# Bits of the first layer's weights in the weight pools' own tiles, values in 128-row tiles, and an order planned with transfers in a row

## The chip, the cores and the metric

The kernel runs on one core of one Trainium2 chip. The metric is the device time of one execution in microseconds, so less is better. Before the change three runs took 1063.34 to 1065.43 us, with a median of 1064.94.

The core has five engines with an instruction stream each: PE (matmuls, with weight loads shown apart as PEld), DVE and ACT (elementwise), POOL, and SP, which in this kernel only issues transfers. Instructions of one engine run in the order in which they were written; engines wait for each other through semaphores.

## What is computed

Linear attention of 4 batches with 8 heads, 576 tokens and 64 columns, and behind it two multilayer perceptrons (MLPs) on its 2304 tokens.

```python
def phi(x):
    proj = np.einsum('bhsd,df->bhsf', x, w_phi)
    proj = proj - np.max(np.abs(proj), axis=-1, keepdims=True)
    return np.concatenate([np.exp(proj), np.exp(-proj)], axis=-1)
q_p, k_p = (phi(q), phi(k))
kv = np.einsum('bhsf,bhsd->bhfd', k_p, v)
z = np.sum(k_p, axis=2)
num = np.einsum('bhsf,bhfd->bhsd', q_p, kv)
den = np.einsum('bhsf,bhf->bhs', q_p, z)[..., None] + 1e-06
x = num / den                               # [2304, 512] after the heads are joined
...
h = x @ w_in                                # first MLP, 512 -> 2048 -> 512
x = (h * (1.0 / (1.0 + np.exp(-h)))) @ w_out
h = np.maximum(x @ w_in, 0.0)               # second MLP, weights of its own
return h * h @ w_out
```

The MLPs' weights come as 64-bit floats.

## The kernel before

**Work.** Heads are taken in pairs, so a batch j has four pairs p. The tokens of a batch are two blocks of 288, eight blocks in all. Each MLP is cut into 16 chunks of 128 hidden columns: for a block i and a chunk c, 12 matmuls make `h` (L887), ACT and DVE turn it into a high and a low half (`gh`, `gl`), and 12 matmuls add to the four accumulators `o` (L932). Layer 0 runs blocks 0 to 7 and layer 1 follows with blocks 0 to 7; names end in layer, block and chunk, so h0_7_0 is layer 0, block 7, chunk 0. In the text "chunk 0" and "chunk 15" without a block are those of layer 0, block 0. Most matmuls use numbers split into a high half, rounded to the format of the faster matmul, and a low half, the remainder (`hi_act` on ACT, L326, and `lo_on`, L330).

**Keys and values** (`keys_of`). The keys `kr` of a pair are projected (`pk`, L560) in five token tiles of KT = 116 rows (the last of 112), grouped as two, two and one. DVE takes the largest magnitude of each row (L565). In batch 0 DVE then subtracts it (`kd`, L571) and ACT takes both exponentials of a whole group (`kp`, L648). In batch 1 ACT negates the maximum (L582) and takes the exponentials straight from the projection, 128 columns at a time with the maximum as bias (L634), and DVE subtracts nothing. Batches 2 and 3 work with split numbers (L593, L621). The values `v` are loaded into columns of a tile in which POOL has first set a column of ones behind each group of 64 (L507, L510): 116 rows of ten pieces of 64 numbers. `pkv` (L664 for batches 0 and 1) is the product with the exponentials, and `kv` its copy.

**Queries** (`queries_of`), for a block and a pair: load `qr` (L730), project (`pq`, L749 to L752), copy to `qp` (L755), reduce over partitions on POOL (L762), subtract (L768), two exponentials `qe` (L780), the product `pn` with kv (L814), copy `qn` (L817), the denominators through three small transfers (`rr` L829, `rd` L836, `qb` L839), and the quotient `x` (L852) with its two halves, the input of the block's chunks.

**Weights** (`w_conv`, `w_split`). Half a chunk of weights, 128 x 1024 words, is loaded into a raw buffer `wr` (L404). ACT takes the magnitude of the upper words (L407), DVE makes the 32-bit number in four steps (L413, L415, L419, L423), and `w_split` writes its halves into the chunk's tile `w`. There are three raw buffers (`NRAW`), shared with the values of batches 2 and 3, and eight tiles `w` in the pool `wp` for chunks 0 to 7; chunks 8 to 15 have the pool `wq`, which opens when the buffers of the first attention close. The second layer's weights are made during blocks 3 to 7 of the first, go out to `w2d` and come back as `w2f`.

**Order.** `Plan` is a list scheduler which runs before the program is written. Each operation has a key (its due time in chunks), a planned duration, and buffers to take and give back; at each moment an engine gets the ready operation with the smallest key that `safe` allows. What comes out is the order in which instructions are written. Keys come from a table (`P`) and from the calls of `want` at the end: `k0s`, `q0s`, `q0`, `w0`, `ws` for the start, `k1`, `k`, `qo`, `qe` for later batches, `W2A`, `W2B` for the second layer's weights. Attention on PE is put ahead of the MLP by 132.7 chunks, and the MLP's work on ACT and DVE ahead of the attention's by 106.06. A transfer is planned as SP's time `max(600, kb * 1024 / 330)` and a latency of 2000 ns. On the chip SP issues all transfers from one queue.

## Time and profile before

| | |
|---|---|
| median of three runs | 1064.94 us |
| the profiled execution | 1062.18 us |
| its span, first to last instruction | 1060.4 us |
| mean granted TensorE clock | 0.977 |
| moved by transfers | 88.39 MB, mean 83 GB/s |
| shortest packets | 30816 of 67387 under 512 bytes |

Views used below: the page's shares and slices; a table of stretches (busy time of each engine between two moments, then the granted clock, the busy share of the 16 DMA engines and GB/s); the timeline (start, duration, engine, line, operation, output and inputs, how many; in brackets the idle time ahead of it and what ended it); groups of instructions by line and shape (count, busy us, mean ns, idle us before them); and waits (who waited for whom: us in all, times, longest). "SPq" is SP's queue of transfers.

### The profile page before, as it was taken

To read this page: it belongs to the slowest core of one execution; us is meant where nothing else is said; L and a number is where in the kernel's file an instruction comes from. 1 tells how busy PE (TensorE), PEld (TensorE's weight loads), DVE (VectorE), ACT (ScalarE), POOL (GpSimd) and SP (SyncE) were. 2 spreads that over 40 slices of the span, in tenths; PEclk is the share of its full clock that TensorE was granted. 3 is DMA by queue.
4 is the path that set the end of the run, shared out by engine and by line. 5 is a ranking of instruction groups with operands and counts; after the bars stand their busy time and mean duration, and the time that the engine had idled before them with its cause. 6 is when DMAs were issued, how large, how long until landed. Compare 5 with 4: busy or idle time off the path is not lost.

```text
span 1060.4 us, 19152 instructions
## 1 busy us (share of the span) xinstructions
PE 1019.5 (96%) x7424; PEld 992.0 (94%) x7424; DVE 629.7 (59%) x1278; ACT 550.0 (52%) x1369; POOL 75.6 (7%) x56
## 2 busy tenths in 40 slices
PE   7879798998999999999999999999999999999998
PEld 5649687998999999999999999999999999999998
DVE  3889879776657756898977688232323233333232
ACT  4755776776867767876644465232323232332222
POOL 2130002120002300031100000000000000000000
PEclk8989988999999999999999999999999999999999
DMA  6455462213201122237355694010101010100000
GB/s 171 109 141 152 134 171 78 74 41 76 61 23 51 54 56 80 74 113 218 112 177 175 215 318 156 1 45 2 45 1 45 2 46 1 46 1 24 1 24 23
DMA packets 67387, 88.39 MB, mean 83 GB/s; under 512 B 30816, under 2 KB 43232, under 8 KB 67296
## 3 DMA queue, kind: packets, MB, share of 16 engines
q1 hardware_dynamic: 67296, 87.17, 27.9%
q8 instruction: 58, 0.95, 0.4%
q14 instruction: 33, 0.27, 0.1%
HBM read 69.17 MB, written 17.90 MB: 82 GB/s over the span
## 4 chain that ended last, share of the span: by engine, by line
PE 74%; DMA 10%; DVE 10%; ACT 3%; issue 2%; SPq 1%; POOL 0%; ACTq 0%; DVEq 0%
PE h L887 32%; PE o L932 32%; DMA wr<-w 3%; PE pn L814 3%; PE pkv L621 2%; DMA qb<-rd 2%; PE pkv L664 1%; DVE wc L419 1%; DVE wc L423 1%; DMA rd<-rr 1%; PE pk L560 1%; ACT kp L634 1%; DMA rr<-qn 1%; DVE x L852 1%; SPq L502 1%
## 5 line engine op out<-in xcount | busy, mean ns | idle before, releaser
L887 PE MATMUL h<-x,w 128*128 128x288 f32 x3072 | 455.1, 297 | 6.7 <-DVE w L330 2.0
L932 PE MATMUL o<-gh,w 128*128 128x288 f32 x2048 | 456.7, 297 | 4.2 <-ACT gh L326 3.4
L887 PEld LDWEIGHTS h<-x,w 128*128 128x128 f32 x3072 | 425.5, 190 | 9.4 <-issue 2.7
L932 PEld LDWEIGHTS o<-gh,w 128*128 128x128 f32 x2048 | 345.6, 189 | 5.7 <-ACT gh L326 4.9
L932 PE MATMUL o<-gl,w 128*128 128x288 f32 x1024 | 303.2, 296 | 1.9 <-DVE gl L330 1.8
L330 DVE TENSOR_TENSOR gl<-a,gh 128x288 fp32r<-128x288 f32 x256 | 122.3, 478 | 167.6 <-ACT gh L326 167.0
L326 ACT CAST gh<-a 128x288 fp32r<-128x288 f32 x256 | 111.7, 437 | 199.0 <-PE o L932 148.7
L932 PEld LDWEIGHTS o<-gl,w 128*128 128x128 f32 x1024 | 193.4, 189 | 2.9 <-DVE gl L330 2.6
L904 DVE TENSOR_TENSOR a<-h,a 128x288 f32<-128x288 f32 x128 | 58.4, 456 | 108.6 <-ACT a L895 108.6
L895 ACT ACTIVATE a<-h 128x288 f32<-128x288 f32 x128 | 52.5, 410 | 117.4 <-PE h L887 117.0
L762 POOL PARTITION_ALL_REDUCE qm<-qp x32 | 73.1, 2303 | 319.2 <-ACT qp L755 178.7
L900 DVE SCALAR_TENSOR_TENSOR a<-a,h 128x288 f32<-128x288 f32 x128 | 57.6, 450 | 29.9 <-ACT a L893 29.2
L407 ACT ACTIVATE wc<-wr 128x512 f32<-128x512 f32 x64 | 43.2, 678 | 46.6 <-DMA wr<-w 46.2
L893 ACT ACTIVATE a<-h 128x288 f32<-128x288 f32 x128 | 53.3, 416 | 12.9 <-PE h L887 12.7
L423 DVE SCALAR_TENSOR_TENSOR wc<-wr,wc 128x512 int32<-128x512 int32 x64 | 46.1, 720 | 0.5
L419 DVE SCALAR_TENSOR_TENSOR wc<-wr,wc 128x512 int32<-128x512 int32 x64 | 45.8, 715 | 0.5
L593 ACT ACTIVATE ke<-pk,mx 116x128 f32<-116x128 f32 (+1 forms) x160 | 46.0, 402 | 0.0
L780 ACT ACTIVATE qe<-qp 128x576 f32<-128x576 f32 x64 | 41.6, 681 | 6.5 <-DVE qp L768 5.3
L664 PEld LDWEIGHTS pkv<-v,kp 116*128 116x128 f32 (+1 forms) x320 | 41.1, 210 | 1.4 <-issue 0.6
L814 PE MATMUL pn<-qh,kv 128*65 128x288 f32 x192 | 41.8, 294 | 0.0
L664 PE MATMUL pkv<-v,kp 116*128 116x128 f32 (+1 forms) x320 | 41.4, 293 | 0.0
L413 DVE TENSOR_SCALAR wc<-wc 128x512 f32<-128x512 f32 x64 | 28.9, 454 | 19.3 <-ACT wc L407 18.9
(83 smaller groups left out, 958.7 us busy)
## 6 DMA issues: line engine op xcount, KB each, us to landing
wr<-w SPq DMA_DIRECT2D x64, 512.0 KB, 5.1
w2d<-wc SPq DMA_DIRECT2D x32, 256.0 KB, 2.9
w2f<-w2d SPq DMA_DIRECT2D x32, 256.0 KB, 4.9
qr<-qT SPq DMA_DIRECT2D x56, 144.0 KB, 3.1
v<-v SPq DMA_DIRECT2D x16, 290.0 KB
kr<-kT SPq DMA_DIRECT2D x16, 288.0 KB, 3.8
qb<-rd SPq DMA_DIRECT2D x32, 144.0 KB, 3.2
x2d<-y SPq DMA_DIRECT2D x32, 144.0 KB, 2.0
```

The lines of the kernel that those rows point to most:

```text
L326: nc.scalar.copy(out=dst, in_=src)
L330: e.tensor_tensor(out=dst, in0=src, in1=hi.bitcast(F32), op=ALU.subtract)
L419: nc.vector.scalar_tensor_tensor(out=b, in0=lo, scalar=29, in1=b, op0=ALU.logical_shift_right, op1=ALU.bitwise_or)
L423: nc.vector.scalar_tensor_tensor(out=b, in0=hi, scalar=-(1 << 30), in1=b, op0=ALU.bitwise_and, op1=ALU.bitwise_or)
L664: nc.tensor.matmul(get(ps)[:, o:o + 128], get(kps[2 * g + s])[:nt, 2 * i + a], get(vt)[:nt, c:c + 128], start=t == 0 and a == 0 and s == 0 ...
L762: nc.gpsimd.partition_all_reduce(get(mx), get(pr).rearrange("p a t -> p (a t)"), 128, bass.bass_isa.ReduceOp.absmax)
L814: nc.tensor.matmul(get(ps)[:D1, :HB], w, get(e)[:, t], start=x == 0, stop=x == len(ops) - 1)
L887: nc.tensor.matmul(get(ps)[:, :HB], a, x[:, cc], start=k == 0, stop=k == 3 * ND - 1)
L893: nc.scalar.activation(out=a, in_=get(ps)[:, :HB], func=AF.Tanh, scale=0.5)
L900: nc.vector.scalar_tensor_tensor(out=a, in0=a, scalar=1.0, in1=get(ps)[:, :HB], op0=ALU.add, op1=ALU.mult)
L904: nc.vector.tensor_tensor(out=a, in0=get(ps)[:, :HB], in1=a, op=ALU.mult)
L932: nc.tensor.matmul(get(acc)[:, :HB], a, g, start=c == 0 and x == 0, stop=c == NC - 1 and x == 2)
```

## The change

*Bits in the weight pools.* For chunks 0 to 4 and 8 to 12 of layer 0 both halves of the raw words land in a tile of the pool that later holds the chunk's `w` (`w_tile("bits", c)`, 128 x 2 x 1024 words, shown as `wbits`). Other halves use raw buffers as before.

*Values.* KT is 128 (the last tile has 64 rows). The host lays v out with room for the ones, one row of 650 numbers for each of 128 partitions; the load is contiguous, and POOL sets the ones behind it.

*Batch 0 without a subtraction.* `bx` = 0 gives batch 0 the path of batch 1 (`direct`).

*Order.* The planner issues a transfer in 640 ns, lets all transfers pass one after the other at 240 bytes per ns, and adds 1500 ns. Loads of keys, and queries behind the keys of their pair, keep their order (`behind`). The keys sit in one table, `KEYS`, with new numbers. Line numbers from 23 on rise by up to 23 (L330 is L337 there, L510 is L531, L560 is L582, L634 is L656).

```diff
 ND = DM // 128
-KT = 116
+KT = 128
 NKT = 5
...
         self.allocs, self.frees, self.state = [], [], 0
+        self.behind = None
...
     LAT = {"PE": 450, "SP": 150}
-    DMA_LAT = 2000
+    DMA_ISSUE, DMA_LAT, DMA_RATE = 640, 1500, 240.0
...
         if unit and engine == "PE":
-            key -= 132.7
+            key -= KEYS["pe"]
         if not unit and engine in ("ACT", "DVE"):
-            key -= 106.06
+            key -= KEYS["el"]
         o = Op(len(self.ops), key, engine, cost, emit, unit)
...
         busy = dict.fromkeys(engines, 0.0)
-        events, now, left = [], 0.0, len(self.ops)
+        events, now, left, dma_free = [], 0.0, len(self.ops), 0.0
         self.active = []
...
                     if e == "SP":
-                        busy[e] = now + o.cost
-                        end = now + o.cost + self.DMA_LAT
+                        busy[e] = now + self.DMA_ISSUE
+                        dma_free = max(dma_free, busy[e]) + o.cost * 1024 / self.DMA_RATE
+                        end = dma_free + self.DMA_LAT
                     else:
...
     def allowed(self, o):
-        return not o.allocs or self.safe(o)
+        return not (o.behind and not o.behind.state) and (not o.allocs or self.safe(o))
...
 def dma(kb):
-    return max(600, kb * 1024 / 330.0)
+    return kb
...
 MM, MM256 = 132, 117
+
+
+KEYS = {
+    "k0s": 6.03, "q0s": 11.22, "q0": 7.53, "w0": 41.79, "ws": 3.48, "we": -10.51, "q1": 19.08, "qo": 5.92,
+    "qs": 0.92, "k1": 29.08, "k": 15.38, "ks": 0.85, "qe": -5.28, "w2a": 51.96, "w2b": 2.48, "bx": 0,
+    "pe": 114.63, "el": 100.63, "wl": 3.76, "kl": 3.74, "vl": -5.21, "ql": 3.88, "g2": 2.17,
+}
...
     nc = tc.nc
-    P = {
-        "k0s": 8.2, "q0s": 5.98, "q0": 7.67, "w0": 36.83, "ws": 3.47, "we": 1.51, "q1": 13.83, "qo": 4.11, "qs": 0.47, "k1": 27.16, "k": 15.28,
-        "ks": 1.3, "qe": 8.44,
-    }
+    P = KEYS
     NT, NRAW, NATT, NG, NU = 14, 3, 2, 3, 4
     NW, NE, NEU = 8, 28, 11
-    W2A, W2B = 51.14, 3.33
+    W2A, W2B = P["w2a"], P["w2b"]
     WARM = 4
-    JF, BX = 2, 1
+    JF, BX = 2, P["bx"]
     EW = 14
+    NWR = 5
     NX, NXK = 1, 2
...
     op(T0 - 99, "DVE", 200, blank, w=["blank"])
-    op(T0 - 99, "SP", dma(128), phi_load, r=["blank"], w=["wraw"])
+    op(T0 - 99, "SP", dma(64), phi_load, r=["blank"], w=["wraw"])
     op(T0 - 99, "POOL", 1500, phi_zero, w=["wbl0", "ident"])
...
         u.early = layer == 0 and 2 * c + part < EW
-        raw = Buf("raw", lambda: rp.tile([128, 512, 2], I32, tag="raw", name="wr" + n), None)
+
+        if layer == 0 and c % (NC - NW) < NWR:
+            raw = w_tile("bits", c)
+            words = lambda: get(raw)[:, part]
+        else:
+            raw = Buf("raw", lambda: rp.tile([128, 2 * 512], I32, tag="raw", name="wr" + n), None)
+            words = lambda: get(raw)
         f = slot("wc" + n, u, (128, 512))
...
         def load():
-            src = (w1, w2)[layer][c, :, part * 512:(part + 1) * 512].bitcast(I32)
-            nc.sync.dma_start(out=get(raw).rearrange("p n two -> p (n two)"), in_=src)
+            nc.sync.dma_start(out=words(), in_=(w1, w2)[layer][c, :, part * 512:(part + 1) * 512].bitcast(I32))
+
+        def halves():
+            return words().rearrange("p (n two) -> p n two", two=2)
         def mag():
-            nc.scalar.activation(out=get(f), in_=get(raw)[:, :, 1].bitcast(F32), func=AF.Abs)
+            nc.scalar.activation(out=get(f), in_=halves()[:, :, 1].bitcast(F32), func=AF.Abs)
...
             t, b = get(f), get(f).bitcast(I32)
-            lo, hi = get(raw)[:, :, 0], get(raw)[:, :, 1]
+            lo, hi = halves()[:, :, 0], halves()[:, :, 1]
             if i == 0:
...
         r = [(("c", 0, hold // NC, hold % NC), "h")] if layer else []
-        op(key - 4, "SP", dma(512), load, r=r, w=[(k, 0)], bufs=[raw])
+        op(key - P["wl"], "SP", dma(512), load, r=r, w=[(k, 0)], bufs=[raw])
         op(key, "ACT", act(512), mag, r=[(k, 0)], w=[(k, 1)], bufs=[raw, f], unit=u)
...
-    def w_split(layer, c, part, f, u, key, engine):
-        k = ("wf", layer, c, part)
-        if part == 0:
+    def w_tile(layer, c):
+        if (layer, c) not in wch:
             first = c < NC - NW
...
                 "w" if first else "wq",
-                lambda: (wp if first else late_pool()).tile([128, 4, 512], F32R, tag="w", name=f"w{layer}_{c}"), None
+                lambda: (wp if first else late_pool()).tile(
+                    [128, 4, 512] if layer in (0, 1) else [128, 2, 1024], F32R if layer in (0, 1) else I32, tag="w",
+                    name=f"w{layer}_{c}"
+                ), None
             )
-        w = wch[layer, c]
+        return wch[layer, c]
+
+    def w_split(layer, c, part, f, u, key, engine):
+        k = ("wf", layer, c, part)
+        w = w_tile(layer, c)
...
-    kvs = {}
+    kvs, loads = {}, {}
...
         def v_load():
-            nc.sync.dma_start(out=values()[:, :, :D], in_=v[j * NP + p].rearrange("k t a d -> k (t a) d"))
+            nc.sync.dma_start(out=get(vt), in_=v[j * NP + p])
...
-        op(key - 4, "SP", dma(288), load, w=[(K, "raw")], bufs=[raw], unit=u)
+        loads[K] = op(key - P["kl"], "SP", dma(288), load, w=[(K, "raw")], bufs=[raw], unit=u)
+        loads[K].behind = loads.get(("k", (j * NP + p - 1) // NP, (p - 1) % NP))
         parts = [raw]
...
                bufs=[raw, hi, lo], unit=u)
-        op(key - 3, "POOL", 200, ones, r=[(K, "raw" if whole else "lo")] if split else [], w=[(K, "one")], bufs=[vt])
-        op(key - 3, "SP", dma(290), v_load, r=[(K, "one")], w=[(K, "v")], bufs=[vt])
+        op(key - P["vl"], "SP", dma(325), v_load, r=[(K, "raw" if whole else "lo")], w=[(K, "v0")], bufs=[vt])
+        op(key - P["vl"], "POOL", 200, ones, r=[(K, "v0")], w=[(K, "v")], bufs=[vt])
...
                 if g == 0:
-                    op(key, "ACT", act(NKT * 2 * D1), v_hi, r=[(K, "v"), "kvs"], w=[(K, "vh")], bufs=[vt] + vs)
+                    op(key, "ACT", act(NKT * 2 * D1), v_hi, r=[(K, "v"), "kvs"] + [("kt", x) for x in range(JF * NP)], w=[(K, "vh")], bufs=[vt] + vs)
                     op(key, "DVE", dve(NKT * 2 * D1), v_lo, r=[(K, "v"), (K, "vh")], w=[(K, "vl")], bufs=[vt] + vs)
...
         else:
-            op(key, "PE", 4 * NKT * 2 * MM256, kv_mm, r=[(K, "v")] + [((K, g), "e", s) for g in range(3) for s in range(2)],
-               w=[(K, "t")], bufs=[ps, kv, vt] + kps, unit=u)
+            op(key, "PE", 4 * NKT * 2 * 113, kv_mm, r=[(K, "v")] + [((K, g), "e", s) for g in range(3) for s in range(2)],
+               w=[(K, "t"), ("kt", j * NP + p)], bufs=[ps, kv, vt] + kps, unit=u)
         if kv_one:
...
-        op(key - 4, "SP", dma(288), load, w=[(Q, "raw")], bufs=[raw], unit=u)
+        op(key - P["ql"], "SP", dma(144 if whole else 288), load, w=[(Q, "raw")], bufs=[raw], unit=u).behind = loads[K]
+        loads[Q] = plan.ops[-1]
         if not whole:
...
-            op(key + 3.18, "PE", 3 * MM, gemm2, r=W + [(C, "gh"), (C, "gl")], w=[("acc", L, i, d)],
+            op(key + P["g2"], "PE", 3 * MM, gemm2, r=W + [(C, "gh"), (C, "gl")], w=[("acc", L, i, d)],
                bufs=[acc, gb, w])
...
     qT = np.asarray(inputs["q"]).reshape(B, NP, 2, 2, HB, D).transpose(0, 3, 1, 5, 2, 4).reshape(B * 2 * NP, D, 2 * HB)
-    vv = np.zeros((B * NP, NKT * KT, 2, D), v.dtype)
-    vv[:, :S] = v.transpose(0, 2, 1, 3)
-    vv = vv.reshape(B * NP, NKT, KT, 2, D).transpose(0, 2, 1, 3, 4)
+    vv = np.zeros((B * NP, NKT * KT, 2, D1), v.dtype)
+    vv[:, :S, :, :D] = v.transpose(0, 2, 1, 3)
+    vv = vv.reshape(B * NP, NKT, KT, 2 * D1).transpose(0, 2, 1, 3).reshape(B * NP, KT, NKT * 2 * D1)
```

The start of SP's queue, before the change (`kr`, `qr`, `v` with batch or block and pair; `wr` with layer, chunk and half):

```order
L502 DMA kr0_0_109<-kT 128x576
L346 DMA wbl_93<-w_phi 64x128 x2
L730 DMA qr0_0_119<-qT 64x576
L510 DMA v0_0_121<-v 116x10x64
L502 DMA kr0_1_126<-kT 128x576
L510 DMA v0_1_123<-v 116x10x64
L730 DMA qr0_1_140<-qT 64x576
L502 DMA kr0_2_147<-kT 128x576
L730 DMA qr0_2_157<-qT 64x576
L502 DMA kr0_3_172<-kT 128x576
L730 DMA qr0_3_182<-qT 64x576
L404 DMA wr0_0_0_196<-w1 128x1024
```

and with it:

```order
L523 DMA kr0_0_109<-kT 128x576
L523 DMA kr0_1_112<-kT 128x576
L353 DMA wbl_93<-w_phi 64x128 x2
L752 DMA qr0_0_121<-qT 64x576
L523 DMA kr0_2_123<-kT 128x576
L523 DMA kr0_3_125<-kT 128x576
L531 DMA v0_0_127<-v 128x650
L752 DMA qr0_1_129<-qT 64x576
L531 DMA v0_1_135<-v 128x650
L752 DMA qr0_2_140<-qT 64x576
L752 DMA qr0_3_149<-qT 64x576
L416 DMA wbits_0_153<-w1 128x1024
```

The keys of all four pairs now stand ahead of the values, and the first bits, five halves in a row, come at the same place in the queue.

ACT's first rows behind the preparation of the projection, before the change (`kp` with batch, pair, group and sign):

```order
L648 ACTIVATE kp0_0_0_0_159<-kd0_0_0_149 116x512
L648 ACTIVATE kp0_0_0_1_165<-kd0_0_0_149 116x512
L755 COPY qp0_0_174<-pq0_0_0_153 128x288
L755 COPY qp0_0_174<-pq0_0_1_161 128x288
L648 ACTIVATE kp0_0_1_0_184<-kd0_0_1_170 116x512
L648 ACTIVATE kp0_0_1_1_190<-kd0_0_1_170 116x512
L648 ACTIVATE kp0_0_2_0_200<-kd0_0_2_177 112x256
L648 ACTIVATE kp0_0_2_1_204<-kd0_0_2_177 112x256
```

and with it:

```order
L604 ACTIVATE mx0_0_0_151<-mx0_0_0_151 128x4
L656 ACTIVATE kp0_0_0_0_160<-pk0_0_0_137,mx0_0_0_151 128x128 x4
L656 ACTIVATE kp0_0_0_1_172<-pk0_0_0_137,mx0_0_0_151 128x128 x4
L604 ACTIVATE mx0_0_1_158<-mx0_0_1_158 128x4
L604 ACTIVATE mx0_0_2_170<-mx0_0_2_170 64x2
L656 ACTIVATE kp0_0_1_0_190<-pk0_0_1_146,mx0_0_1_158 128x128 x4
L656 ACTIVATE kp0_0_1_1_198<-pk0_0_1_146,mx0_0_1_158 128x128 x4
L656 ACTIVATE kp0_0_2_0_211<-pk0_0_2_155,mx0_0_2_170 64x128 x2
L656 ACTIVATE kp0_0_2_1_216<-pk0_0_2_155,mx0_0_2_170 64x128 x2
```

Each exponential of a group became four, or two, with a negation ahead, and the copies of the first query moved behind the exponentials of pair 1.

DVE's rows around the end of block 6 of layer 0, from the last low half of block 7's x on; before the change, where the row of its chunk 0 stands 76 rows further on:

```order
L330 TENSOR_TENSOR x1_7_6945<-x7_3_7005,x0_7_6944 128x288
L423 SCALAR_TENSOR_TENSOR wc1_7_0_6958<-wr1_7_0_6908,wc1_7_0_6958 128x512
L330 TENSOR_TENSOR gl0_6_0_7023<-a0_6_0_7021,gh0_6_0_7022 128x288
L413 TENSOR_SCALAR wc1_7_1_6996<-wc1_7_1_6996 128x512
L415 TENSOR_SCALAR wc1_7_1_6996<-wc1_7_1_6996 128x512
L900 SCALAR_TENSOR_TENSOR a0_6_1_7060<-a0_6_1_7060,h0_6_1_7008 128x288
L419 SCALAR_TENSOR_TENSOR wc1_7_1_6996<-wr1_7_1_6947,wc1_7_1_6996 128x512
```

and with it, where that row is among these:

```order
L337 TENSOR_TENSOR x1_7_7001<-x7_3_7662,x0_7_7000 128x288
L337 TENSOR_TENSOR gl0_6_14_7657<-a0_6_14_7655,gh0_6_14_7656 128x288
L438 SCALAR_TENSOR_TENSOR wc1_15_1_7646<-wr1_15_1_7575,wc1_15_1_7646 128x512
L923 SCALAR_TENSOR_TENSOR a0_6_15_7696<-a0_6_15_7696,h0_6_15_7673 128x288
L337 TENSOR_TENSOR gl0_6_15_7698<-a0_6_15_7696,gh0_6_15_7697 128x288
L923 SCALAR_TENSOR_TENSOR a0_7_0_7731<-a0_7_0_7731,h0_7_0_7712 128x288
L337 TENSOR_TENSOR x1_8_7739<-x2r0_0_7693,x0_8_7738 128x576
L337 TENSOR_TENSOR gl0_7_0_7733<-a0_7_0_7731,gh0_7_0_7732 128x288
```

The conversions of the second layer (`wc1`, `w1`) that stood between the two rows have moved ahead of the first.

## The prediction

> **What bounds the kernel now.** I read the page first: the shares of the engines, then the slices.
>
> ```profile
> PE 1019.5 (96%) x7424; PEld 992.0 (94%) x7424; DVE 629.7 (59%) x1278; ACT 550.0 (52%) x1369; POOL 75.6 (7%) x56
> ...
> PE   7879798998999999999999999999999999999998
> ...
> DVE  3889879776657756898977688232323233333232
> ```
>
> PE is busy for 96% of the span, but the slices show two stages: up to the seventh or eighth slice of 26.5 us PE has holes while DVE is at 7 to 9 tenths, and after that PE has none. The table by stretches says how much is to be had in each.
>
> ```profile
> 0.00:82.00 82.00, 65.52 (x309) 48.09 (x310) 56.26 (x113) 46.15 (x100) 19.63 (x22) 0.85 0.53 139
> 82.00:186.00 104.00, 91.06 (x588) 84.19 (x587) 89.83 (x179) 71.35 (x195) 7.45 (x5) 0.91 0.45 134
> 186.00:300.00 114.00, 110.78 (x841) 110.24 (x840) 78.83 (x159) 82.86 (x224) 11.56 (x9) 0.99 0.24 59
> 300.00:600.00 300.00, 296.63 (x2258) 294.18 (x2256) 226.32 (x452) 195.72 (x494) 37.00 (x20) 1.00 0.38 113
> 600.00:1060.00 460.00, 455.53 (x3438) 455.30 (x3437) 178.47 (x379) 153.94 (x357) 0.00 (x0) 1.00 0.15 49
> ```
>
> Columns are the length, then busy PE, PEld, DVE, ACT, POOL, the granted clock, DMA share and GB/s. PE is idle for 16.5 us before 82, 12.9 us up to 186, and after that for 3.2, 3.4 and 4.5 us, the last at the very end of the program. So the span is the time of chunk 15 of the first block, the point where this front ends, plus a row of matmuls that hardly waits. What sets that point is read from the instructions around it.
>
> ```profile
> 82.14 0.44 DVE L900 SCALAR_TENSOR_TENSOR a<-a,h 128x288 f32<-128x288 f32 x1
> ...
> 182.34 0.68 DVE L330 TENSOR_TENSOR w<-wc,w 128x512 fp32r<-128x512 f32 x1
> ...
> 186.15 0.44 DVE L900 SCALAR_TENSOR_TENSOR a<-a,h 128x288 f32<-128x288 f32 x1
> ```
> ```profile
> 183.62 4.94 PE L887 MATMUL h<-x,w 128*128 128x288 f32 x36
> ```
>
> The weight half that chunk 15 needs ends on DVE at 183.02, and 0.6 us later its matmuls start and run on without a gap. 82.14 and 186.15 are DVE's first instruction on chunk 0 and on chunk 15. **DVE is the bound of the front**: it must convert all sixteen chunks of w1 beside the attention, and it is idle for 25.7 us before 82 and 14.2 us after. Everything below is counted at these two instructions.
>
> **The change, part by part.** *No subtraction in batch 0.* It takes twelve DVE instructions away and gives ACT exponentials of 128 columns for those of 512 and 256.
>
> ```profile
> L571 DVE TENSOR_TENSOR kd<-pk,mx 116x512 f32<-116x512 f32 x8 | 5.5, 685 | 0.1
> L571 DVE TENSOR_TENSOR kd<-pk,mx 112x256 f32<-112x256 f32 x4 | 1.6, 406 | 0.0
> ```
> ```profile
> 22.81 1.15 ACT L648 ACTIVATE kp<-kd 116x512 f32<-116x512 f32 x2 [0.91 <-DVE kd L571]
> ...
> 109.17 0.19 ACT L582 ACTIVATE mx<-mx 116x4 f32<-116x4 f32 x1
> 109.39 2.17 ACT L634 ACTIVATE kp<-pk,mx 116x128 f32<-116x128 f32 x8
> ```
>
> DVE loses 5.5 + 1.6 = 7.1 us. On ACT eight short exponentials take 2.17 us where two long ones took 1.15, and a negation of 0.2 us comes before them: +1.2 us for a group of two tiles, and about half of it for the last tile, so +3.1 us for a pair and +12.4 us for four, all of it before chunk 0.
>
> *Loads.* The loads of v occupy the transfers far longer than their size.
>
> ```profile
> 57.25 0.70 SPq L510 DMA_DIRECT2D v<-v  x1
> 58.34 4.59 SPq L829 DMA_DIRECT2D rr<-qn  x1
> ```
> ```profile
> 243.00:247.00 4.00, 4.00 (x34) 4.00 (x32) 1.38 (x2) 0.70 (x2) 0.00 (x0) 1.00 0.28 48
> ```
> ```profile
> kr<-kT SPq DMA_DIRECT2D x16, 288.0 KB, 3.8
> ```
>
> Behind a v the next issue stands for 4.59 us where it takes 0.5 otherwise, and while v alone is on the way (243 to 247) only 0.28 of the DMA engines are busy, at 48 GB/s. In 128 rows of 2600 bytes v has the form of the keys, 288 KB in 3.8 us, so I take the stalls as gone. What they cost the bound is bounded by who waits:
>
> ```profile
> ACT wc L407 <- DMA wr<-w: 25.8, 15, 4.1
> ```
> ```profile
> SPq L404 <- DVE wc L423: 59.5, 18, 6.5
> ```
> ```profile
> DVE wc L413 <- ACT wc L407: 6.6, 5, 4.6
> ```
> ```profile
> 11.03 3.48 PE L560 MATMUL pk<-wbl,kr 128*116 128x256 f32 x10 [2.47 <-DMA kr<-kT]
> ```
>
> In the first 200 us ACT waits 25.8 us for weight bits (15 times, 4.1 at most), and SP 59.5 us for DVE to give a raw buffer back. With five more tiles in each pool the first loads are queued without such a wait, so a load no longer stands behind the conversion that frees its buffer. The 25.8 us are ACT's, though, and DVE, which is the bound, waited for those ACT instructions for 6.6 us; PE waited 2.47 us for the second keys, which were queued behind the first v. Their worth lies between nothing and DVE's whole idle time in the front, 40 us; I take it in the two stretches below, nearer to nothing. The memset of the ones now stands behind v's landing on POOL, which costs POOL's next reduction up to one landing, 3.8 us, and nothing where POOL is idle (19.6 of 82 us busy). The tiles of 128 keys are five as before, with as many matmuls; time goes with columns in these rows (685 ns for 512, 406 for 256), so that edit costs nothing, and the planner's new rules add no instruction, only order.
>
> *Up to chunk 0.* The new order puts more in front of it: on DVE 16 conversion steps, 3 low halves of w, 2 subtractions of a query and 4 small ones more, and 12 kd fewer.
>
> ```profile
> L413 DVE TENSOR_SCALAR wc<-wc 128x512 f32<-128x512 f32 x64 | 28.9, 454 | 19.3 <-ACT wc L407 18.9
> ...
> L423 DVE SCALAR_TENSOR_TENSOR wc<-wr,wc 128x512 int32<-128x512 int32 x64 | 46.1, 720 | 0.5
> ...
> L768 DVE TENSOR_TENSOR qp<-qp,qm 128x576 f32<-128x576 f32 x32 | 26.7, 840 | 5.7 <-POOL qm L762 5.6
> ...
> L330 DVE TENSOR_TENSOR w<-wc,w 128x512 fp32r<-128x512 f32 x32 | 22.7, 709 | 2.5 <-ACT w L326 2.4
> ```
>
> Half the steps cost 454 and half 720 ns: 9.4 us; with 2.1 for w (709 each), 1.7 for the subtractions, 1.3 for the small ones and 7.1 off, DVE has 7.4 us more, 63.7 us. Its idle time I work out by place. Until its first reduction, at 10.07, nothing changes (about 9 us idle):
>
> ```profile
> 10.07 0.69 DVE L565 TENSOR_REDUCE mx<-pk 116x4 f32<-116x512 f32 x1
> ```
>
> Then it has seven reductions (0.69 us each, the two of half the width 0.4: 4.3) and waits for ACT, whose row now begins with both first pairs: 40 exponentials by 0.27 us, 6 negations, 2 copies of a query and the first magnitude from 11 us on, so to about 24.6: 10 us idle.
>
> ```profile
> L407 ACT ACTIVATE wc<-wr 128x512 f32<-128x512 f32 x64 | 43.2, 678 | 46.6 <-DMA wr<-w 46.2
> L780 ACT ACTIVATE qe<-qp 128x576 f32<-128x576 f32 x64 | 41.6, 681 | 6.5 <-DVE qp L768 5.3
> ...
> L755 ACT COPY qp<-pq 128x288 f32<-128x288 f32 x64 | 24.1, 403 | 8.1 <-PE pq L752 4.6 <-PE pq L749 3.0
> ```
>
> The magnitude is 0.68 and a copy 0.4 us in these rows. The 32 exponentials of pairs 2 and 3 (8.7 us) stand ahead of the next magnitudes in the same way; I allow 4 us. 63.7 + 23 = **87 us**, 5 later than 82.
>
> *Chunk 0 to chunk 15.* By the orders DVE has 273 instead of 289 instructions before chunk 15: the 12 kd, one low half of a query, two subtractions of a query and one low half of w fewer, 10.2 us. As 7.4 us more stand before chunk 0, 17.6 us fewer stand between. Neighbours overlap a little, so 16 us of busy time: 89.8 - 16 = 74, and with 13 us idle, about as before, 87. PE allows no less than 85: its 91.1 us lose 8 matmuls of pn (4.2 us) to the time before chunk 0 and 11 others (1.5 us) to the time after. Chunk 15 comes at 87 + 87 = 174 instead of 186: **-12**. The 1.5 us are paid later.
>
> *Behind it.* The stalls after v go here too; the holes around them are within the 3.2 us of PE, of which I take 1. Against it stands the order of blocks 5 and 6. From the first chunk of block 5 to that of block 7 DVE has 231 instructions instead of 188, and the last low half of block 7's x stands five rows before DVE's first instruction on that block's chunk 0, where it stood 76 rows before it.
>
> ```profile
> 440.00:490.00 50.00, 49.88 (x380) 49.45 (x380) 42.83 (x83) 36.38 (x89) 11.45 (x5) 1.00 0.43 125
> 490.00:540.00 50.00, 48.60 (x359) 47.35 (x359) 43.28 (x91) 29.79 (x69) 7.29 (x3) 1.00 0.54 161
> ```
> ```profile
> 524.41 0.29 PE L814 MATMUL pn<-qo,kv 128*65 128x288 f32 x1
> ```
> ```profile
> 546.40 0.45 DVE L330 TENSOR_TENSOR x<-x,x 128x288 fp32r<-128x288 f32 x1
> ```
>
> Today 22 us lie between the last pn of block 7 (524.7) and its x (546.9), and some 45 us are left. In the new order about 160 matmuls, 21 us, stand between that pn and block 7. Two blocks last some 112 us: their 768 matmuls by 0.133 us (36 in 4.94 us, less the last one's end) are 102, and the new order has about 15 us of attention between them, so 117. DVE, busy for 86.1 us in the 100 of these rows, comes to about 96 in such a length, and 43 instructions by 0.49 us (629.7 by 1278 on the page) make it 110 to 117. At 94% busy or more PE loses nothing; at the 86% of these rows 117 us would last 128 or longer, 11 us lost; I take 4, with 0 and 11 kept for the range.
>
> **The sum**: -12 + 1.5 - 1 + 4 = -7.5 us on the span. The profiled execution took 1062.18 us (span 1060.4), 2.8 under the median 1064.94; I put the difference on the median: **1057 us**.
>
> **Rivals.** *More gain.* If loads that are always there take DVE's gaps, chunk 0 stays at 82 and the stretch sinks to PE's 85.4: chunk 15 at 167.5, -18.6 + 1.5 - 1, and blocks 5 to 7 lose nothing: 1047. For it speaks that 25.8 us of ACT's waits are for exactly these loads; against it that ACT now opens with 11 us of exponentials. *Hidden anyway.* DVE was the bound, and what ACT and SP waited for was not: then only part of the 7 us of kd is won, and the late blocks take it back: 1065, within 0.2%. It would also be the case if the queue of transfers, now filled with 512 KB loads, delayed the small ones of the reciprocals. *Slower: ACT becomes the bound of the start.* Before chunk 0 ACT has 46.2 us; the exponentials add 12.4, and 16 moved instructions (four each of magnitudes, halves of w, exponentials and evacuations, 0.4 to 0.68 us) 9.5: 68 us. Today it is idle for 36 us of the 82; if its waits in turn with DVE stay that long, chunk 0 comes at 104, 17 us after my 87: 1074. It decides from chunk 0 at about 96 on, where the gain is gone. Against it: 13.9 of those 36 us were waits for loads that now land early, by the first of these rows.
>
> ```profile
> ACT wc L407 <- DMA wr<-w: 13.9, 5, 4.1
> ```
> ```profile
> 71.20 4.10 PE L814 MATMUL pn<-qe,kv 128*65 128x288 f32 x8 [5.60 <-ACT qe L780]
> ```
>
> One more way to the slow side is the matmul clock. The row of 0 to 82 has it at 0.85, with a hole of 5.6 us in PE just before chunk 0, and the new front has more attention and no chunk in that time. The Trainium skill ("TensorE: Matmul & The Clock Gate", Part 1) says that about 3.4 us without work set the array to half rate. If half rate held all through the start, PE's 65.5 us and the 4.2 of pn would become (65.5 + 4.2) x 0.85 / 0.5 = 118 us, and the time 1088. The measured 0.85 speaks against it; I give it 2 in 100 and count it with the slower side.
>
> **How the numbers follow.** Forecast 0.52 (its own range 1052 to 1062), more gain 0.18, hidden 0.13, slower 0.17. Within 0.2% is 1062.8 to 1067.1, about what a measurement can tell from no change. That makes faster 0.70, same 0.13, slower 0.17. The range goes from the better rival with 3 us of margin, 1044, to 1070, where chunk 0 comes near 100; most of the slower side is left out.
>
> **What would show it.** Right: no kd on DVE, DVE waiting for ACT at 13 to 24 us, its first instruction on chunk 0 near 87 and on chunk 15 near 174, ACT's waits for weight bits under 10 us in the first 200, no issue of 3 us or more behind a v, and DMA shares above 0.5 while v moves. Wrong: chunk 0 after 96 with ACT busy throughout, chunk 15 after 180, or PE idle for more than 10 us between 400 and 620, with the x of block 6 or 7 as what it waits for.

## The result and the profile after

The changed kernel takes **1039.70 us** (median of 4 runs, 1038.46 to 1040.52) beside 1065.18 of the kernel before in the same comparison: a ratio of **0.9754, with a 95% interval of 0.9722 to 0.9786**. The forecast was 1057 with a range of 1044 to 1070, so the direction was right and the size was not: the gain is 25 us where 8 were forecast, and the time lies below the range. The profiled execution has a span of 1037.5 us, 22.9 less than before. The ratios in this document leave out a single run, one of ten of bits_in_old_plan, which took 1986.39 us where its other nine took 1065.88 to 1071.74.

The page of the changed kernel, first the shares, then the slices (now 25.9 us each):

```profile
PE 1011.4 (97%) x7424; PEld 979.5 (94%) x7424; DVE 626.6 (60%) x1266; ACT 558.9 (54%) x1437; POOL 82.2 (8%) x56
...
PE   8679999999999999999999999999999999999998
...
DVE  3898998888568656898998675232333333333322
...
PEclk9799999999999999999999999999999999999999
```

From the fourth slice to the last but one PE is busy for at least nine tenths, where it fell below that in five of the first seven and in the tenth; its granted clock is lowest, 0.7, in the second slice. DVE is as busy as before. The two instructions on which the prediction counts, DVE's first on chunk 0 and on chunk 15 of the first block:

```profile
87.36 0.41 DVE L923 SCALAR_TENSOR_TENSOR a<-a,h 128x288 f32<-128x288 f32 x1
...
167.47 0.46 DVE L923 SCALAR_TENSOR_TENSOR a<-a,h 128x288 f32<-128x288 f32 x1
```

The table of stretches of the changed kernel, cut at these two moments and at the first chunk of the second layer (length; busy PE, PEld, DVE, ACT, POOL; clock, DMA share, GB/s):

```profile
0.00:87.36 87.36, 69.74 (x329) 47.43 (x330) 65.72 (x126) 63.85 (x185) 22.05 (x20) 0.88 0.50 153
87.36:167.47 80.11, 78.68 (x564) 73.54 (x563) 72.70 (x150) 59.35 (x173) 2.82 (x5) 1.00 0.46 153
167.47:624.30 456.83, 454.62 (x3459) 450.43 (x3458) 352.23 (x699) 313.05 (x792) 57.33 (x31) 1.00 0.40 118
624.30:1037.50 413.20, 408.36 (x3081) 408.13 (x3079) 135.95 (x292) 122.64 (x291) 0.00 (x0) 1.00 0.08 23
```

The kernel before, cut at its own chunk 15 and its own second layer:

```profile
186.15:647.00 460.85, 454.26 (x3450) 451.26 (x3449) 344.51 (x692) 308.70 (x784) 48.56 (x29) 1.00 0.39 115
647.00:1060.40 413.40, 408.53 (x3084) 408.30 (x3082) 138.96 (x298) 123.67 (x292) 0.00 (x0) 1.00 0.08 24
```

Chunk 15 comes 18.7 us earlier than before (186.15), and the rest of the program is 4.2 us shorter, 870.0 instead of 874.2 us. In the stretch from chunk 0 to chunk 15 PE is idle for 1.4 us where it was for 12.9, at a clock of 1.00 where it was 0.91. Between chunk 15 and the second layer PE is idle for 2.2 us where it was for 6.6.

### The profile page after: what moved, and what is told of

Read it like the earlier page. It is cut to its first block, busy times and chain, and to the rows that moved or that the text cites. A ratio compares the mean times of both kernels' runs of the same rounds, so it can differ in the third digit from the quotient of the medians.

```text
span 1037.5 us, 19194 instructions
## 1 busy us (share of the span) xinstructions
PE 1011.4 (97%) x7424; PEld 979.5 (94%) x7424; DVE 626.6 (60%) x1266; ACT 558.9 (54%) x1437; POOL 82.2 (8%) x56
## 4 chain that ended last, share of the span: by engine, by line
PE 85%; DVE 7%; ACT 3%; issue 2%; DMA 2%; POOL 0%; SPq 0%; POOLq 0%; ACTq 0%; DVEq 0%
PE o L955 37%; PE h L910 37%; PE pn L837 4%; PE pk L582 3%; PE pkv L643 2%; PE pkv L686 2%; ACT kp L656 2%; DVE wc L434 1%; DVE wc L438 1%; DMA wr<-w 1%; DVE wc L428 1%; DVE w L337 1%; DVE wc L430 1%; DMA qb<-rd 1%; DVE qp L791 0%
## 5 line engine op out<-in xcount | busy, mean ns | idle before, releaser
L910 PE MATMUL h<-x,w 128*128 128x288 f32 x3072 | 449.6, 295 | 0.3 <-ACT qn L840 0.2
L337 DVE TENSOR_TENSOR gl<-a,gh 128x288 fp32r<-128x288 f32 x256 | 122.2, 478 | 79.5 <-ACT gh L333 62.1
L785 POOL PARTITION_ALL_REDUCE qm<-qp x32 | 79.3, 2499 | 311.7 <-ACT qp L778 171.8
L615 ACT ACTIVATE ke<-pk,mx 128x128 f32<-128x128 f32 (+1 forms) x160 | 44.6, 384 | 0.0
L656 ACT ACTIVATE kp<-pk,mx 128x128 f32<-128x128 f32 (+1 forms) x160 | 43.9, 396 | 0.4
L686 PEld LDWEIGHTS pkv<-v,kp 128*128 128x128 f32 (+1 forms) x320 | 37.5, 193 | 3.3 <-issue 1.6
L337 DVE TENSOR_TENSOR qo<-qe,qh 128x576 fp32r<-128x576 f32 x48 | 39.0, 819 | 2.7 <-ACT qh L333 2.5
L686 PE MATMUL pkv<-v,kp 128*128 128x128 f32 (+1 forms) x320 | 39.2, 280 | 1.2 <-issue 1.2
L875 DVE TENSOR_TENSOR x<-qn,qb 64x288 f32<-64x288 f32 x64 | 32.0, 499 | 7.9 <-DMA qb<-rd 7.4
```

Of the source, the lines that this page charges most:

```text
L337: e.tensor_tensor(out=dst, in0=src, in1=hi.bitcast(F32), op=ALU.subtract)
L656: nc.scalar.activation(out=get(kp)[:nt, x], in_=get(ps)[:nt, x * F:(x + 1) * F], func=AF.Exp, scale=1.0 - 2.0 * s, bias=get(mx)[:nt, s, x: ...
L686: nc.tensor.matmul(get(ps)[:, o:o + 128], get(kps[2 * g + s])[:nt, 2 * i + a], get(vt)[:nt, c:c + 128], start=t == 0 and a == 0 and s == 0 ...
L785: nc.gpsimd.partition_all_reduce(get(mx), get(pr).rearrange("p a t -> p (a t)"), 128, bass.bass_isa.ReduceOp.absmax)
L910: nc.tensor.matmul(get(ps)[:, :HB], a, x[:, cc], start=k == 0, stop=k == 3 * ND - 1)
```

## The experiments

The change has four parts that can be had apart: the loads of v in 128 rows, the places for bits in the weight pools, batch 0 without kd, and the new planner with its table of keys. A part that touches only what an instruction does leaves the planned order as it is; the other parts make the planner order anew. In all diffs `...` stands for lines left out.

### v back, and v alone

**v_pieces_in_new**, order of the changed kernel:

```diff
-KT = 128
+KT = 116
...
-            nc.sync.dma_start(out=get(vt), in_=v[j * NP + p])
+            nc.sync.dma_start(out=values()[:, :, :D], in_=v[j * NP + p].rearrange("k t a d -> k (t a) d"))
```

> The changed kernel with the values as before: 116-row tiles, ten pieces of 64 numbers a row; the order of all instructions is that of the changed kernel. Theory L (the loads of v cost the front and block 2 their stalls): SP's issue behind each v stands 3.5 to 5.5 us again, and the time comes back by a good part, 1045 to 1055, with PE idle again near the loads of batch 1. Theory O (raw tiles and the order did it, and a slow v is hidden by loads that are queued early): 1039 to 1043.

Measured: 1041.12 us, ratio 0.9781 (0.9759 to 0.9802), in theory O's range. SP does stand behind v again (rows of it are below). Chunk 15 comes 4.0 us later than in the changed kernel, at 171.5, but the blocks behind it are shorter, and 1.4 us of the medians is left.

**v_rows_in_old**, the same edit the other way in the kernel before, with its order (the ones move behind the load, the values come in rows that have room for them, and the token tiles of the keys get 128 rows too):

```diff
-KT = 116
+KT = 128
...
-            nc.sync.dma_start(out=values()[:, :, :D], in_=v[j * NP + p].rearrange("k t a d -> k (t a) d"))
+            nc.sync.dma_start(out=get(vt), in_=v[j * NP + p])
+            nc.gpsimd.memset(values()[:, :, D:], 1.0)
```

> The kernel before with only its v changed: 128-row tiles loaded in one row of 2600 bytes, ones set behind the load; the order is that of the kernel before. Theory L: the 3.2 us of PE's idle time at 240 us and some of the front's holes go, 1050 to 1058. Theory O: 1060 to 1065, since the raw buffers still wait for DVE and the order leaves DVE's holes where they were. DMA share while v moves: above 0.5 in both.

Measured: **1046.31 us, ratio 0.9828 (0.9809 to 0.9846)**, 18 us of gain from this edit alone, more than either theory had. So v's loads are worth 18 us in one order and 1 to 3 in the other: neither theory holds for both. How it comes about in the old order can be read from SP's queue at the start, the same eight issues in each. The kernel before:

```profile
3.31 0.83 SPq L510 DMA_DIRECT2D v<-v  x1
4.18 3.75 SPq L502 DMA_DIRECT2D kr<-kT  x1
7.98 0.68 SPq L510 DMA_DIRECT2D v<-v  x1
8.70 4.36 SPq L730 DMA_DIRECT2D qr<-qT  x1
...
14.27 0.58 SPq L502 DMA_DIRECT2D kr<-kT  x1
```

and v_rows_in_old:

```profile
3.30 0.59 SPq L510 DMA_DIRECT2D v<-v  x1
3.93 0.43 SPq L502 DMA_DIRECT2D kr<-kT  x1
4.40 0.43 SPq L510 DMA_DIRECT2D v<-v  x1
4.88 0.47 SPq L731 DMA_DIRECT2D qr<-qT  x1
...
6.54 0.58 SPq L502 DMA_DIRECT2D kr<-kT  x1
```

The keys of the fourth pair are issued 7.7 us earlier, and DVE's first instruction on chunk 0 comes at 73.5 instead of 82.1, 8.7 us earlier. Chunk 15 gains 2.7 more (174.8), and block 1, where PE's 3.2 us of holes go, 5.5 more: its stretch is 67.9 us long, not 73.45.

### Rows or pieces

v_rows_in_old changes the count of rows and the length of the pieces together. Two kernels change one each, in the order of before. **v_116_whole** is v_rows_in_old with

```diff
-KT = 128
+KT = 116
```

> The kernel before, its order kept, v still in 116-row tiles but each row loaded in one piece of 2600 bytes. Two things changed together in v_rows_in_old (1046.3): the count of rows and the length of the pieces. Theory R (the count of rows decides over how many of the 16 DMA engines a load spreads): DMA share stays near 0.3 while v moves, SP still stands behind it, 1058 to 1065. Theory P (256-byte pieces are what was slow): as v_rows_in_old, 1045 to 1050.

Measured: 1060.14 us, ratio 0.9968 (0.9953 to 0.9984). **v_128_pieces** is the kernel before with `KT = 128` and nothing else.

> The kernel before, its order kept, v in 128-row tiles but in ten pieces of 256 bytes a row. Theory R: DMA share above 0.5 while v moves and 1045 to 1050. Theory P: no better than before, 1060 to 1066.

Measured: 1046.93 us, ratio 0.9847 (0.9820 to 0.9873). Theory R holds: the rows decide. KT is the height of the keys' tiles as well, but their work isn't what got faster: the median matmul of `pk` takes 379 ns and of `pkv` 275 ns with 116 rows and with 128, and a subtraction of 512 columns 685 and 681 ns. Two microseconds in which little but loads of v is on the way (length, clock, DMA share, GB/s), of before, v_116_whole, v_128_pieces and v_rows_in_old in this order:

```profile
264.00:266.00 2.00, 1.00 0.34 62
```
```profile
263.00:265.00 2.00, 1.00 0.26 101
```
```profile
245.00:247.00 2.00, 1.00 1.08 242
```
```profile
245.00:247.00 2.00, 1.00 0.79 297
```

With 116 rows the busy share is about a quarter to a third of the 16 DMA engines, with 128 rows 0.79 and 1.08. The longer piece raises what is moved (62 to 101 GB/s), but not the share. The Trainium skill ("DMA: Bandwidth & Descriptors", "Why a DMA increments its semaphore by 16 and not by 1") says that a transfer runs on the largest number of engines, at most 16, that divides the slowest dimension on both sides. Worked out from that rule, this is 4 for 116 rows and 16 for 128. The shares agree, 0.26 and 0.34 being a little above 4/16.

v_116_whole shows one thing more: there SP no longer stands behind a v (the next issues come 0.4 to 0.6 us apart), and still only 3 to 4 us are gained, none of them in the front: chunk 0 comes at 86.8 and chunk 15 at 189.1, later than in the kernel before. What is late there is what the transfers bring. The keys of the second pair are issued behind the first v at 3.87, and PE waits for them until 12.20; v_rows_in_old issues them at 3.93, and PE starts on them at 9.37 without a wait. First v_116_whole, then v_rows_in_old:

```profile
12.20 2.42 PE L561 MATMUL pk<-wbl,kr 128*116 128x256 f32 x10 [2.71 <-DMA kr<-kT]
```
```profile
9.37 2.57 PE L561 MATMUL pk<-wbl,kr 128*128 128x256 f32 x10
```

The standing issue was what one saw; the late landing of v, and of the loads issued behind it, was what it cost.

### The places for bits

**raw_buffers_only** is the changed kernel, planned anew, with

```diff
-    NWR = 5
+    NWR = 0
```

> The changed kernel without bits in the weight pools (every half through the three raw buffers, planned anew). Theory B (the extra places for bits are what lets the front run): chunk 0 of block 0 on DVE later than 92 or chunk 15 later than 175, ACT waits above 15 us for bits in the first 190 us, time 1048 to 1060. Rival (order and key table): the planner finds as good an order, 1038 to 1045.

Measured: 1048.91 us, ratio 0.9860 (0.9834 to 0.9887). Chunk 0 comes at 89.5 and chunk 15 at 179.6, 12.1 us later than in the changed kernel. Half of theory B fails: ACT does not wait for bits (3.5 us in the first 186). As the order was planned anew, the 9 us are what the places and the order made for them are worth together.

**bits_in_old_plan** puts the code of the changed `w_conv` and `w_split` into the kernel before, with `NWR = 5` and the old planner and keys; it also takes over the changed kernel's rules on the buffers of v (the ones behind the load, and the split of v in batches 2 and 3 behind all products of batches 0 and 1). **bits_and_v_in_old_plan** has 128 rows of v besides.

> The kernel before (v in 116-row pieces, old planner, old table, kd on DVE) with bits of five chunks in each weight pool. The places alone, if raw buffers held the front up: SP's loads of bits before the slow v's, 1045 to 1055. If the stalls behind v are what costs, and places alone can't pass them: 1060 to 1066.

> As bits_in_old_plan, with v in 128 rows of 2600 bytes. If the gains of v and of the places add (18.5 for v alone, 9 for the places in the new order): 1037 to 1040. If they take away the same waits: 1043 to 1048, and what is left of the change's gain is its order and its exponentials.

Measured: 1068.97 us, ratio 1.0046 (1.0023 to 1.0070), and 1050.15 us, ratio 0.9868 (0.9835 to 0.9901). In the old plan the places, together with these rules, lose 4 to 5 us, with slow and with fast loads of v.

### kd, the order, and what takes v off the path

**subtract_again** is the changed kernel, planned anew, with this entry of its table:

```diff
-"bx": 0
+"bx": 1
```

> The changed kernel with the subtraction kd of batch 0 back on DVE (planned anew). If DVE's 7.1 us of kd were what bounds the front: chunk 15 about 7 us later and 1045 to 1048. If they fell into DVE's idle time before chunk 0 (21.6 us in the changed kernel): within 3 us of 1039.7.

Measured: 1043.65 us, ratio 0.9802 (0.9781 to 0.9823): about 4 us more, between the two expectations. Chunk 0 comes earlier, at 79.1, where ACT has 49.0 us of work ahead of it instead of 63.9, and chunk 15 later, at 172.2.

**plan_alone** has the new planner and table, and the rest as before: `NWR = 0`, `"bx": 1`, v in 116 rows of pieces (only the changed kernel's rules on the buffers of v stay).

> The changed kernel's planner and table with everything else as before: v in 116-row pieces, bits through the three raw buffers, kd on DVE. Theory S (the new order issues v and keys so early that a slow v holds nothing up): 1045 to 1052, about raw_buffers_only (1048.9) although v is slow. Rival (the order helps only with fast loads or the places): 1058 to 1068.

Measured: 1060.41 us, ratio 0.9962 (0.9947 to 0.9977). Theory S fails: the order alone doesn't hide a slow v. Which part of the change does was then asked by three more runs. **sub_pieces** and **raw_pieces** are subtract_again and raw_buffers_only with v in 116 rows of pieces, their orders kept, and **plan_rows** is plan_alone with 128 rows of 2600 bytes.

> subtract_again (new planner and table, places for bits, kd on DVE; 1043.65) with v back in 116-row pieces, order the same. The slow v costs 18.5 us in the old order and 1.4 in the new one. Theory P (the places for bits are what makes room: what stands behind a v has time in hand): about 1 to 5 more, 1045 to 1049. Theory E (the exponentials on ACT are what takes v off the path): 1055 to 1062.

> raw_buffers_only (new planner and table, no kd, no bits in the weight pools; 1048.9) with v back in 116-row pieces, order the same. Theory P: without the places the slow v costs 8 us or more, 1057 to 1066. Theory E: 1 to 4 more, 1050 to 1053.

> plan_alone (new planner and table, no places, kd on DVE, v in pieces; 1060.4) with v in 128 rows, order the same: closes the table. If the new order alone, with fast loads, is worth something beyond v: below 1046.3 (v_rows_in_old). If not: 1046 to 1050.

Measured: 1062.10 (0.9957, 0.9934 to 0.9981), 1059.13 (0.9919, 0.9890 to 0.9948) and 1044.59 us (0.9784, 0.9753 to 0.9816). All ratios to before, measured beside it on the same chip, by order and by form of v; a thousandth is about 1.06 us, and a worth is uncertain by up to some 4 us:

| order | v in 116 rows of pieces | v in 128 whole rows | worth of v |
|---|---|---|---|
| before | 1 | 0.9828 | 18 us |
| before, with places for bits | 1.0046 | 0.9868 | 19 us |
| new planner and table alone | 0.9962 | 0.9784 | 19 us |
| and without kd | 0.9919 | 0.9860 | 6 us |
| and with places for bits, kd kept | 0.9957 | 0.9802 | 16 us |
| all (the change) | 0.9781 | 0.9754 | 3 us |

Among the new orders, v is worth 19 and 16 us in those that keep kd, and 6 and 3 in those without it; the places change that by 3 us only. So theory P falls: sub_pieces has the places and pays 16 us. Theory E has the right side but not the size: raw_pieces takes 1059.13 us, not 1050 to 1053. This doesn't show that kd is the cause, as each of these orders was planned anew, and they lose time at different places. At chunk 15 plan_alone is already 8.3 us behind plan_rows (186.0 and 177.7). sub_pieces is only 1.4 us behind subtract_again there, where all of kd's work is done, and loses the rest from 245 us on. There SP, ACT and PE of sub_pieces have these rows:

```profile
245.69 11.10 SPq L531 DMA_DIRECT2D v<-v  x3
256.85 9.38 SPq L975 DMA_DIRECT2D x2d<-y  x4
```
```profile
264.93 0.41 ACT L970 ACTIVATE y<-o 128x288 f32<-128x288 f32 x1 [9.25 <-DMA x2d<-y]
```
```profile
265.40 0.61 PE L955 MATMUL o<-gh,w 128*128 128x288 f32 x1 [9.07 <-ACT y L970]
```

Three v's in a row take 11.1 us to issue; the four stores of a finished block stand behind them, ACT waits 9.25 us for a store to free its buffer, and PE waits 9.07 us for ACT to empty an accumulator. This is about half of the 21 us by which this profiled execution, the longest of its ten, is behind that of subtract_again; the other half lies in smaller holes. In subtract_again the same three are issued in 1.28 us:

```profile
244.09 1.28 SPq L531 DMA_DIRECT2D v<-v  x3
```

In v_pieces_in_new the order has the v's of that place apart, with the stores between two of them. At the start queries stand behind its first two v's, and bits behind the next two:

```profile
253.66 6.07 SPq L975 DMA_DIRECT2D x2d<-y  x4
259.82 0.70 SPq L531 DMA_DIRECT2D v<-v  x1
```
```profile
30.25 0.70 SPq L531 DMA_DIRECT2D v<-v  x1
31.00 9.39 SPq L416 DMA_DIRECT2D wbits<-w  x2
```

The stall of 9.39 us is there, and chunk 0 is only 0.5 us later than with fast loads. What a slow load of v costs in these rows depends on what stands behind it. For the other orders of the table this wasn't followed up.

### The clock

Matmuls run faster in the changed kernel's front. Twelve matmuls of `h` behind a hole of the kernel before, and twelve without a hole in the changed one:

```profile
137.72 2.57 PE L887 MATMUL h<-x,w 128*128 128x288 f32 x12 [2.01 <-DVE w L330]
```
```profile
91.07 1.76 PE L910 MATMUL h<-x,w 128*128 128x288 f32 x12
```

**fill_holes_in_old** asks whether that is a cost of its own. The extra matmuls go to unused columns of banks in which sums of block 0 are open, and the output is a different one, so this kernel stands here for its time alone. `FILL` is 14.

```diff
+        def fill(ps):
+            for _ in range(FILL if (L, i) == (0, 0) else 0):
+                nc.tensor.matmul(
+                    get(ps)[:, HB:], wbl_hi[:, 0], wbl_hi.rearrange("p a f -> p (a f)")[:, :512 - HB], start=True,
+                    stop=True, skip_group_check=True,
+                )
...
+            if c == 10:
+                fill(ps)
...
+                if d == 0 and c in (9, 12, 13):
+                    fill(acc)
```

> The kernel before with 14 extra matmuls of 224 columns, into unused columns, at each of four places where PE waits about 2 us (ahead of the product of chunk 9, of h of chunk 10, of the products of chunks 12 and 13): about 1.5 us of work in each hole, the order kept. It asks whether the low clock behind holes is a cost of its own. Theory C (a hole costs twice, since the matmuls behind it run slower): the granted clock of 126 to 186 us goes to 1.0 and the time falls by 3 to 6 us, 1058 to 1062. Theory D (DVE is the bound there, a slow PE lies beside it): the clock rises, the time stays within 2 us of 1064.

Measured: 1062.61 us, ratio 0.9988 (0.9969 to 1.0008). Two stretches of before, and of fill_holes_in_old:

```profile
126.00:150.00 24.00, 19.98 (x120) 18.41 (x119) 18.21 (x38) 17.16 (x56) 0.30 (x1) 0.86 0.51 144
162.00:186.00 24.00, 20.22 (x129) 19.54 (x130) 23.13 (x38) 16.34 (x42) 7.03 (x3) 0.86 0.25 79
```
```profile
126.00:150.00 24.00, 20.62 (x141) 19.31 (x140) 17.83 (x37) 17.05 (x55) 0.12 (x1) 0.93 0.45 130
162.00:186.00 24.00, 21.40 (x161) 20.28 (x162) 22.91 (x39) 16.34 (x43) 7.94 (x3) 1.00 0.25 79
```

The clock rises from 0.86 to 0.93 and 1.00, and chunk 15 still comes at 186.0. Theory D holds: in the second stretch DVE, busy for 23 of 24 us, sets the pace, and a slow PE lies beside it. So in the order of before the low clock cost nothing that shows, and its return alone gains nothing. In the changed kernel PE is busy for 78.68 of the 80.11 us from chunk 0 to chunk 15, so a low clock may well be paid for there; no run tests that.

### A try at beating both

**replan_measured** is the changed kernel with other durations and keys for its planner (a key that isn't shown is unchanged or moved by less than 0.5; the exponentials of batches 2 and 3 are planned with 275 too):

```diff
-    op(key, "ACT", 2 * m * act(F, True) - 180, ex, ...
+    op(key, "ACT", 2 * m * 275, ex, ...
...
-    op(key, "PE", 4 * NKT * 2 * 113, kv_mm, ...
+    op(key, "PE", 4 * NKT * 2 * 127, kv_mm, ...
...
-    "k0s": 6.03, "w0": 41.79, "ks": 0.85, "bx": 0, "wl": 3.76, "ql": 3.88
+    "k0s": 9.6, "w0": 46.89, "ks": 2.23, "bx": 1, "wl": 6.49, "ql": 3.13
```

> A try at beating both: the changed kernel planned with the durations that its trace shows (four exponentials of 128 columns 1.1 us where the plan counts 0.69, a pair's product with v 5.1 us where it counts 4.5), kd of batch 0 back on DVE, and the table of keys set anew for these durations. If ACT's uncounted 8 us in the start are what keeps chunk 0 at 87: chunk 0 before 82, chunk 15 before 165, 1033 to 1038. If the start is bound by chains of waits that no table sees: 1039 to 1045.

**changed_again** is the changed kernel itself, beside it.

> The changed kernel as it is, beside replan_measured on one chip: 1038 to 1041.

Measured on one chip: replan_measured 1040.52 us, ratio 0.9772 (0.9756 to 0.9788); the changed kernel again 1039.33 us, ratio 0.9760 (0.9742 to 0.9778). No difference can be told, and the time is in the second of the two ranges. Chunk 0 does come earlier, at 83.7, but chunk 15 at 166.8 is only 1.4 us before that of the changed kernel beside it (168.2), and the blocks behind give more than that back. Nothing tried beats the changed kernel.

## Why the prediction missed

*Up to chunk 0: right.* 87 was forecast and 87.36 measured; DVE's 63.7 us of work there are 65.72, its 23 us of idle time 21.6. DVE first waits for ACT where it was expected, 5.9 us at most, and ACT's waits for bits fell from 25.8 us to 1.4:

```profile
DVE wc L428 <- ACT wc L422: 8.9, 2, 5.9
```
```profile
ACT wc L422 <- DMA wr<-w: 1.4, 3, 0.5
```

*Chunk 0 to chunk 15: wrong by 6.9 us.* The stretch takes 80.1 us, not 87. Two steps of the working failed together. "13 us idle, about as before" took DVE's idle time over from the old order; it is 7.4 us. Of the 6.8 us that went, 3.6 are one wait, that for the small transfer of the reciprocals (`qb`): 4.6 us in this stretch before, 1.0 with the change. In the kernel before, the `qb` that DVE waits for is issued behind a v and the two loads of keys that stand behind that v. v_pieces_in_new has the slow v and the wait again. First the kernel before, then two rows of v_pieces_in_new:

```profile
135.60 0.91 DVE L852 TENSOR_TENSOR x<-qn,qb 64x288 f32<-64x288 f32 x2 [3.54 <-DMA qb<-rd]
```
```profile
93.93 6.76 SPq L862 DMA_DIRECT2D qb<-rd  x1
```
```profile
103.56 0.92 DVE L875 TENSOR_TENSOR x<-qn,qb 64x288 f32<-64x288 f32 x2 [3.91 <-DMA qb<-rd]
```

And the floor that forbade less, "PE allows no less than 85", was worked from 91.1 us of busy time at a granted clock of 0.91. PE now does this stretch in 78.68 us of busy time at 1.00; 91.1 by 0.91 would have given 83 before the moved matmuls, and 77 after them. A busy time under a lowered clock is no amount of work. With PE idle for only 1.4 us of this stretch and DVE for 7.4, PE is now the fuller of the two.

*Behind chunk 15: the sign was wrong.* 4.5 us were to be lost and 4.2 were won. Of the 11 matmuls, 1.5 us, that were to move behind it, the rows show six (6540 where there were 6534), and PE's busy time there grows by 0.2 us. The holes of PE up to the second layer shrank by 4.4 us where "I take 1" was written; 3.2 of the 6.6 were in block 1, and v_rows_in_old, with its loads of v alone, has none there. And the 4 us for blocks 5 to 7 are not there:

```profile
454.80:573.40 118.60, 117.49 (x883) 116.68 (x883) 106.70 (x232) 68.00 (x156) 15.71 (x5) 1.00 0.66 193
```
```profile
569.68 0.45 DVE L337 TENSOR_TENSOR x<-x,x 128x288 fp32r<-128x288 f32 x1
```
```profile
571.13 1.08 PE L910 MATMUL h<-x,w 128*128 128x288 f32 x7
```

The two blocks last 118.6 us (117 were forecast), and the last half of block 7's x does end only a microsecond before its chunk 0. But DVE's work is 106.7 us, not 110 to 117, and PE stands for 1.1 us in all: just in time cost nothing here.

*What lies behind the sizes.* The sum gave v's loads no term of their own: "I take it in the two stretches below, nearer to nothing". v_rows_in_old puts 18 us on them in the order of before, so this was mis-sized. The row was at hand, 0.28 of the DMA engines at 48 GB/s while v alone moved; what was not drawn from it is that loads issued behind such a v land late too. Who waits for a load by name said little about it: at the start PE waits 2.47 us for keys and 2.57 for queries, and chunk 0 gains 8.7 us. But the slow v is not all that was missed. v_pieces_in_new keeps it and still gains 23 us, so the new order, the places and the missing kd reach nearly the same without fast loads. Of these, the order alone gains 4 us with a slow v, the order without kd 9, the order with the places 5, and all three 23 (0.9962, 0.9919, 0.9957 and 0.9781). Why they gain so much more together is not shown.

*The rivals.* "More gain" named chunk 15 at 167.5, measured 167.47, but by luck: chunk 0 came at 87.4, not 82, and the stretch took 80.1 us, not 85.4. "Slower" by ACT didn't come: ACT has 63.85 us of the forecast 68 before chunk 0. The half clock didn't either: 0.88 before chunk 0. The Trainium skill ("TensorE: Matmul & The Clock Gate", Part 1) speaks of about 3.4 us without work. The row at 137.72 shows slow matmuls behind a hole of 2.01 us, with another of 2.02 us some 6 us before it:

```profile
131.63 0.58 PE L932 MATMUL o<-gh,w 128*128 128x288 f32 x1 [2.02 <-ACT gh L326]
```

From 132 to 134 us the granted clock is 0.50. So shorter holes lower it here too, and fill_holes_in_old shows that this need not cost time.

*Open.* With v in 128 rows the orders lie between 0.9754 and 0.9868. The change is ahead of its planner and table alone (0.9784) by 3 us, within the intervals, so that the worth of the places and of the missing kd, taken together on top of these, isn't settled.

## What to carry to other kernels

Price a load by the rows over which it is spread, and read that from the share of the DMA engines while it moves alone: 128 rows instead of 116 gave 18 us here, with more bytes (320 KB for 290). Then look at what stands behind a slow transfer in its queue, since the same loads cost 18 us in one order and 3 in another. Multiply a busy time by its granted clock before it is used as a floor.

## What the runs showed of the hardware

- While little but loads of v moves: 116 rows, DMA share 0.26 to 0.34, 62 GB/s in pieces of 256 bytes and 101 in pieces of 2600; 128 rows, 1.08 and 0.79, 242 and 297 GB/s.
- Three such loads in pieces from 116 rows held SP's issues for 11.10 us, three in 128 whole rows for 1.28.
- Twelve matmuls of 288 columns took 2.57 us behind a hole of 2.01 us, and 1.76 us without one. The granted clock was 0.50 in the two microseconds after a hole of 2.02 us.
